# GpSimd's load queue in source order, and the projection products of the last three blocks one product later

## The chip, the core and the metric

The kernel runs on one core of one Trainium2 chip. A core has a TensorE (matrix products), a VectorE and a ScalarE (element by element work; the profile calls them DVE and ACT), a GpSimd (POOL), a SyncE (SP) and 16 DMA engines that all queues share. The metric is the time of one execution in microseconds, the median of several runs; lower is better.

## The reference

Attention over a sliding window, and then a gated feed-forward layer over its output. Shapes: 8 batches, 8 heads, 576 positions, head size 64; model width 512, inner width 1536.

```python
scores = 1/sqrt(64) * q @ k.T                       # each batch and head
mask = (rel >= 0) & (rel < 128)                     # rel = query position - key position
scores = where(mask, scores - slope[h] * abs(rel), -1e9)
attn = softmax(scores)
x = (attn @ v) as [8 * 576, 512]
out = (silu(x @ w_gate) * (x @ w_val)) @ w_out      # [4608, 512], float32
```

Inputs and output are float32.

## The kernel before

**Attention tiles.** The kernel works on 36 tiles of 128 positions, nine for each pair of batches: eight of 128 positions of one batch, and a ninth of the last 64 positions of both. Their number is called rank for inputs and i for work (`units`). For each tile, k, q and v are loaded with a conversion to float16 by DMAs that GpSimd issues (`load_qk` L187, `load_v` L182); the ninth tile of a pair takes two DMAs for each. From rank 11 on, k and q are transposed by DMAs of SyncE's queue (`transpose` L237, L243) into `kT` (12 places) and `qT` (9 places). `scores` makes the products of q and k (L282, L317), ScalarE the exponentials, VectorE applies masks; `weighted` multiplies with v (L349) and divides. Tile i's `weighted` needs v of i and mostly of i-1; the ninth tile also uses v of the fourth and the eighth. Loads of k and q pass through five buffers each (`nat`), which come free when the tile in them has been transposed; v has 12 places.

**What sets the order of loads.** The first eleven ranks are loaded by a list (L880 to L910), which mixes in the weights; after that, `loads_to(i + 7)` is called in tile i (L859), and `load` issues k, q, v for ranks below 10 and v, k, q after that. That is the order in the source. A planner then orders the instructions of each engine by its own costs and due times, except where `tc.manual_schedule` says that an engine's instructions stay in source order. Before, that holds for TensorE, VectorE and ScalarE in the first tiles, and for TensorE from step 60 on. GpSimd's and SyncE's queues are ordered by the planner. An engine takes its queue in order: an instruction that waits holds up all behind it. In GpSimd's queue the planner had put, for example, v of tiles 12, 13, 14 and 16 ahead of k of 12, v of 15 behind k of 23, and v of 33 at the very end.

**Feed-forward blocks.** Nine blocks n = 0 to 8 of 512 rows follow the attention in an interleaved way. Gate and value products of blocks 0 to 5 are plain (L401). For blocks 6 to 8 (`SEVEN_FROM`) each group of columns, a unit u = 0 to 5, takes seven half-size products instead of eight (`gate_val_by_seven`, L615, products at L627, in the banks gX, gY, gZ), with sums of x and weights made by VectorE (L489 to L492 for x, L601 to L604 for weights). `seven_steps` (L683) gives their order: in each unit first, seventh (of the unit before), fifth, sixth, fourth (of the unit before), second, third. A block has 42 such steps, k = 0 to 41. VectorE's adds L663 (after third) and L670 (after seventh) and its products L664 and L679 make hT, the block's inner activations.

**Projection.** The output product of blocks 1 to 8 is made by seven products as well (`strassen` L508, products at L536), twice for each block (t = 0, 1), so 14 steps of six matmuls of 256 columns: A11, A12, S2, S1, S3, S4, A22. Their sums of hT (S2, S3, S4 and S1 in place) are made by VectorE (`sums`, L489 to L492) from the finished hT. The projection of block n-1 is spread over block n: in blocks 7 and 8 (and for block 5's projection in block 6) one step follows each gate/value step with k % 3 == 1 (L753). The last block's own projection comes at the end (`ends`), its first step at k = 41. SyncE stores the results (`store`, L447) from eight `osb` buffers.

## Time and profile before

| What | Value |
|---|---|
| Median of 5 runs | 346.85 us (346.49 to 349.39) |
| The profiled execution's own time | 346.54 us |
| Its span in the profile | 344.8 us |
| TensorE matmul busy | 330.3 us, 96% |
| VectorE busy | 277.2 us, 80% |
| ScalarE busy | 207.6 us, 60% |
| GpSimd busy (issuing loads) | 109.9 us, 32% |
| Software DMA queue (q0), GpSimd's loads | 118336 packets, 18.62 MB, 84.0% of 16 engines |
| Hardware DMA queue (q1) | 40976 packets, 17.64 MB, 29.4% |

How to read it: busy time is the time in which an engine had an instruction in work; matmuls overlap, so their busy time can hide short waits, and the time from one matmul's start to the next tells more. A row of a timeline is: start in us from the start of the span, duration, engine, line, operation, output<-inputs, partitions x elements, and how many alike; in brackets, how long the engine had been idle before it and what ended that. GpSimd counts as busy while it issues a DMA; the transfer itself comes later.

### The profile page before, as it was taken

What the parts mean: (1) busy time and instruction counts of PE and PEld (TensorE: products, weight loads), DVE (VectorE), ACT (ScalarE), POOL (GpSimd) and SP (SyncE); (2) the same over time, 40 slices, a digit from 0 to 9 for tenths busy, and PEclk for the clock granted to TensorE, in tenths of its full rate; (3) what the DMA queues carried; (4) which work ended last, traced back from release to release, by engine and by line L of the source; (5) the groups of instructions that cost most, each with busy time, mean ns of one, the idle gap of its engine ahead of it and who ended that gap; (6) DMA issues with size and microseconds to landing.
All of it is one profiled execution on the core that took longest, in us unless ns stands there. A gap on an engine that the chain in (4) does not pass through costs nothing.

```text
span 344.8 us, 7788 instructions
## 1 busy us (share of the span) xinstructions
PE 330.3 (96%) x2983; PEld 218.7 (63%) x2983; DVE 277.2 (80%) x652; ACT 207.6 (60%) x412; POOL 109.9 (32%) x136
## 2 busy tenths in 40 slices
PE   7999989999999999999999999999999999999995
PEld 4484444444456565566565655565788878878884
DVE  6578885999798669998899999999855875775583
ACT  3758675465766665666555547563477667766750
POOL 8968695258558455634710000000000000000000
PEclk9999999999999999999999999999999999999999
DMA  9999999999999999999999312021101101011014
GB/s 152 169 180 175 159 176 167 103 138 138 158 146 144 170 172 136 178 124 177 151 164 165 94 29 80 15 63 47 63 7 56 63 0 64 20 43 63 0 64 122
DMA packets 160037, 37.37 MB, mean 108 GB/s; under 512 B 147328, under 2 KB 155648, under 8 KB 160000
## 3 DMA queue, kind: packets, MB, share of 16 engines
q0 software_dynamic: 118336, 18.62, 84.0%
q1 hardware_dynamic: 40976, 17.64, 29.4%
q10 hardware_dynamic: 688, 0.62, 0.6%
q8 instruction: 23, 0.38, 0.5%
q14 instruction: 14, 0.11, 0.1%
HBM read 37.91 MB, written 9.44 MB: 137 GB/s over the span
## 4 chain that ended last, share of the span: by engine, by line
PE 58%; DVE 22%; DMA 8%; ACT 6%; issue 4%; POOL 1%; SPq 0%; ACTq 0%; DVEq 0%; POOLq 0%
PE po L536 13%; PE pg L401 11%; PE pv L401 11%; PE gX L627 6%; PE av L349 3%; DVE hT L431 3%; PE gY L627 3%; DMA wo_sb<-in_moe_w_out_dram 3%; DVE uu L420 3%; PE ps L282 2%; DMA kT<-kn 2%; PE p L536 2%; DMA va<-in_v_dram 2%; DVE S L489 2%; DVE hT L490 2%
## 5 line engine op out<-in xcount | busy, mean ns | idle before, releaser
L401 PE MATMUL pv<-xT,wv_sb 128*128 128x512 f16 (+2 forms) x320 | 76.5, 358 | 0.6 <-DVE uu L420 0.3
L401 PE MATMUL pg<-xT,wg_sb 128*128 128x512 f16 (+2 forms) x320 | 75.8, 358 | 0.3 <-DVE xT L377 0.2
L419 ACT ACTIVATE tt<-pg 128x512 f16<-128x512 f32 (+2 forms) x70 | 41.3, 590 | 50.9 <-PE pg L401 49.9
L288 ACT ACTIVATE ex<-ps 128x512 f16<-128x512 f32 x96 | 50.0, 604 | 11.5 <-PE ps L282 11.5
L420 DVE SCALAR_TENSOR_TENSOR uu<-tt,pg 128x512 f16<-128x512 f16 (+2 forms) x69 | 45.9, 666 | 10.4 <-ACT tt L419 10.2
L431 DVE TENSOR_TENSOR hT<-uu,pv 128x512 f16<-128x512 f16 (+2 forms) x70 | 46.7, 666 | 3.6 <-PE pv L401 1.6
L191 POOL DMA_DIRECT2D kn<-in_k_dram x39 | 33.2, 854 | 34.7 <-DMA kT<-kn 24.2
L401 PEld LDWEIGHTS <-wg_sb 128*128 128x128 f16 x320 | 28.2, 98 | 24.4 <-issue 2.6
L401 PEld LDWEIGHTS <-wv_sb 128*128 128x128 f16 x320 | 28.3, 98 | 24.1 <-issue 3.0
L536 PEld LDWEIGHTS <-hT 128*128 128x128 f16 x384 | 36.9, 98 | 9.9 <-issue 1.1
L185 POOL DMA_DIRECT2D va<-in_v_dram x40 | 34.1, 856 | 16.4 <-PE av L349 7.2
L191 POOL DMA_DIRECT2D qn<-in_q_dram x39 | 33.3, 857 | 17.3 <-DMA qT<-qn 6.7
L536 PEld LDWEIGHTS <-S 128*128 128x128 f16 x288 | 27.6, 98 | 11.4 <-DVE S L491 2.6
L294 DVE TENSOR_TENSOR ex<-ex,m_reg 128x1024 f16<-128x1024 f16 x42 | 28.7, 687 | 3.2 <-ACT ex L288 3.1
L352 DVE TENSOR_TENSOR x<-av,rec 128x256 f16<-128x256 f32 x72 | 28.5, 420 | 0.4
L536 PE MATMUL po<-T,S 128*128 128x256 f16 x192 | 26.7, 273 | 1.5 <-DVE S L491 1.5
L536 PE MATMUL po<-T,hT 128*128 128x256 f16 x192 | 26.0, 273 | 0.0
L679 DVE TENSOR_TENSOR hT<-s,v 128x512 f16<-128x512 f16 x18 | 7.6, 423 | 21.4 <-ACT s L678 21.4
L321 ACT ACTIVATE exc<-psc 128x512 f16<-128x512 f32 x40 | 21.3, 607 | 3.7 <-PE psc L317 3.7
L349 PEld LDWEIGHTS <-ex 128*128 128x128 f16 x384 | 17.6, 97 | 5.4 <-issue 2.1
L349 PE MATMUL av<-va,ex 128*128 128x65 f16 x384 | 19.6, 193 | 1.3 <-ACT ex L288 0.7
L282 PE MATMUL ps<-qT,kT 64*128 64x256 f16 x192 | 16.6, 272 | 0.4 <-DVE qT L227 0.2
(134 smaller groups left out, 536.5 us busy)
## 6 DMA issues: line engine op xcount, KB each, us to landing
out_dram<-osb SPq DMA_DIRECT2D x32, 256.0 KB, 2.9
va<-in_v_dram POOLq DMA_DIRECT2D x32, 128.0 KB, 8.7
qn<-in_q_dram POOLq DMA_DIRECT2D x31, 128.0 KB, 8.0
kn<-in_k_dram POOLq DMA_DIRECT2D x31, 128.0 KB, 7.5
wg_sb<-in_moe_w_gate_dram POOLq DMA_DIRECT2D x6, 256.0 KB, 7.5
wv_sb<-in_moe_w_val_dram POOLq DMA_DIRECT2D x6, 256.0 KB, 8.1
wo_sb<-in_moe_w_out_dram POOLq DMA_DIRECT2D x2, 768.0 KB, 9.0
kn<-in_k_dram POOLq DMA_DIRECT2D x8, 64.0 KB, 9.9
```

The lines of the kernel that those rows point to most:

```text
L185: nc.gpsimd.dma_start(va[rank][p0:p1, :, 0:D], src)
L191: nc.gpsimd.dma_start(t_[p0:p1], src)
L288: nc.scalar.activation(e[:, o:o + 2, :], banks[q4][par], AF.Exp, scale=scale)
L294: nc.vector.tensor_mul(e[:, o, :], e[:, o, :], reg[:, o, :])
L349: nc.tensor.matmul(av[:, j, :], w, val, start=(n == 0), stop=(n == len(todo) - 1))
L352: nc.vector.tensor_mul(x[:, 4 * half:4 * half + 4, :], av[:, :, 0:D], rec.broadcast_to([P, 4, D]))
L401: nc.tensor.matmul(ps[:, c0:c1], w[:, kb, ms], xT[n][:, kb, c0:c1], start=(kb == 0 and c0 == 0), stop=(kb == NKB - 1 and c1 == 512), skip_ ...
L419: nc.scalar.activation(tt, pg[:, c0:c1], AF.Tanh, scale=0.5)
L420: nc.vector.scalar_tensor_tensor(out=uu, in0=tt, scalar=one if (n, m) == PIN else 1.0, in1=pg[:, c0:c1], op0=ALU.add, op1=ALU.mult)
L431: nc.vector.tensor_mul(hT[n][:, m, c0:c1], acted[(n, m)][1][:, c0:c1], pv[:, c0:c1])
L536: nc.tensor.matmul(dst, a[:, m, cols], b[:, m, :], start=(start and m == 0), stop=(m == HM - 1), skip_group_check=True)
L627: nc.tensor.matmul(dst[:, i, :], w[:, kb, c0 + i * P:c0 + (i + 1) * P], a[:, kb, :], start=(start and i == 0 and kb == 0), stop=(i == 1 an ...
```

## The change

Two parts. First, GpSimd's queue is put under `manual_schedule` from the first load on, so its DMAs stay in source order, and `load` issues k, q, v for every rank. With that, in GpSimd's queue each tile's loads stand together: v of 15 directly behind k and q of 15, and so on to v of 35 at the end; among the first eleven ranks only v of 0 and k of 2 change places, and v of 11 stands behind k and q of 11. SyncE's queue remains the planner's, which now alternates k and q transposes more strictly and places the stores differently between them. Second, the projection's steps in blocks 6 to 8 follow the gate/value steps with k % 3 == 2, one product later than before. The planner gives VectorE and ScalarE a slightly different order in these blocks. Nothing is added or removed: every engine has the same instructions.

```diff
     def load(rank):
-        if rank < 10:
-            load_qk(rank)
-            load_v(rank)
-        else:
-            load_v(rank)
-            load_qk(rank)
+        load_qk(rank)
+        load_v(rank)
...
             yield 0.5
-            if k % 3 == 1 and k < 42:
+            if k % 3 == 2 and k < 42:
                 next(parts)
                 yield 0.75
...
+    queue = ExitStack()
+    queue.enter_context(tc.manual_schedule(engines={ET.Pool}))
     load_qk(1, "qk")
     load_qk(2, "q")
...
     everything()
+    queue.close()
```

Order at the turn from block 6 to 7, TensorE, before: A22 of the projection before, third (6,5), first (7,0), seventh (6,5), A11, fifth, sixth, fourth (6,5), A12, second, third, first (7,1), S2, seventh (7,0), fifth, sixth, S1, fourth (7,0). After: third (6,5), A22 of the projection before, first (7,0), seventh (6,5), fifth, A11, sixth, fourth (6,5), second, A12, third, first (7,1), seventh (7,0), S2, fifth, sixth, fourth (7,0), S1.

## The prediction

> **What bounds the kernel now.** I read the page first, then who waited for whom on TensorE, then the chain of waits around the waits that the change can touch, then the timelines there. The page:

> ```profile
> span 344.8 us, 7788 instructions
> ...
> PE 330.3 (96%) x2983; PEld 218.7 (63%) x2983; DVE 277.2 (80%) x652; ACT 207.6 (60%) x412; POOL 109.9 (32%) x136
> ...
> DMA  9999999999999999999999312021101101011014
> ```

> TensorE is the bound, but its 96% hides short waits, so I use start-to-start times of matmuls: six of 256 columns take 0.66 us, four take 0.44, and what is longer is a stall. The DMA engines are full until about 190 us, the end of the loads. So the load queue matters only before 190, and only where a load arrives after TensorE wants it. All waits of TensorE for a DMA or for VectorE that lie in the change's reach:

> ```profile
> PE po L536 <- DVE S L491: 1.5, 3, 0.7
> ...
> PE av L349 <- DMA va<-in_v_dram: 0.6, 2, 0.3
> PE gX L627 <- DVE v L670: 0.6, 3, 0.2
> ```

> The columns are total us, times, longest. None exceeds a microsecond: little can be won. The timeline of TensorE places the two waits for v:

> ```profile
> 108.84 0.19 PE L349 MATMUL av<-va,ex 128*128 128x65 f16 x1
> 109.38 0.61 PE L349 MATMUL av<-va,ex 128*128 128x65 f16 x15 [0.34 <-DMA va<-in_v_dram]
> ...
> 165.79 0.61 PE L349 MATMUL av<-va,ex 128*128 128x65 f16 x15 [0.30 <-DMA va<-in_v_dram]
> ```

> A matmul of 65 columns follows the one before after 0.03 us, so the stalls are 109.38-108.84-0.03 = 0.51 us and, likewise from 165.29, 0.47 us. The chain of waits tells which counts:

> ```profile
> 92.20 7.60 DMA kT<-kn
> ...
> 102.93 6.41 DMA va<-in_v_dram
> ...
> 109.38 0.61 PE av L349 x15
> ...
> 163.66 1.00 ACT exc L321 x2
> ...
> 166.02 0.69 DVE exc L325
> ```

> The first v wait is on the chain, the second is not: there ScalarE's exponentials hold VectorE and the chain goes past the matmul. Counting TensorE's weighted sums, tile 15 starts at 108.84. Its v was issued at 102.93 only, because it stood in GpSimd's queue behind k tiles that waited for transposes. Tile 24 (165.29) is the same case.

> **Part A, the load queue.** It removes and adds no transfer; it puts 128 KB issues in the order k, q, v of each tile. The queue's timeline before:

> ```profile
> 59.50 0.88 POOL L185 DMA_DIRECT2D va<-in_v_dram  x1 [0.55 <-PE pv L401]
> 66.99 1.76 POOL L191 DMA_DIRECT2D kn<-in_k_dram  x2 [6.61 <-DMA kT<-kn]
> ...
> 102.93 2.65 POOL L185 DMA_DIRECT2D va<-in_v_dram  x3
> ...
> 180.09 0.89 POOL L185 DMA_DIRECT2D va<-in_v_dram  x1 [6.95 <-PE av L349]
> ```

> (1) v of 15 moves from 102.93 to behind q of 15, about 75 us: its buffer is that of tile 3, last read by tile 8's weighted sums at 67.19. Its stall goes: -0.51. v of 24 moves from 153.71 to just behind tile 17's sums (122.1), 43 us before its use. That stall goes too, but the chain passes elsewhere: I take -0.1, bounds 0 and -0.47.

> (2) What pays: k of 12 waits for the transpose of k of 11, and everything is queued behind it. Before, q of 12 and v of 12, 13, 14 and 16 went ahead of that wait (51.8 to 59.5); now they stand behind it. First to be missed is q of 12, read at 78.56 by scores. Before, the transpose was issued at 60.48 and held k of 12 until 66.99, with six younger loads in flight. Now only q and v of 11 are younger. The page has a transpose of 2.4 us with nothing beside it (`xT<-x`), so I take 59.6+2.4 to 3 = 62.0 to 62.6. [...] Then k of 12 at 62.5, q of 12 at 63.4 (0.87 an issue), landing 3.8 later (the least a kn load took is 3.4), its transpose issued behind k's (1.3 each on SP) at 67.8, landing 5 to 6 later (the first transpose's 5.9): 73 to 74, 5 us before use. [...] Cost 0. If k's transpose still ends at 66.4, q of 12 is ready at 78 to 79.5: a stall up to 1 us; with the worst qT landing, 9.8, about 83: 4.6.

> (3) Tiles 14 to 16 follow 1.3 to 2 us apart per transfer pair; read at 88.52, 94.75 and 99.78, they come at about 82, 86 and 90. Cost 0.

> (4) Head-of-line later: v of 24 waits for 122.1 and v of 33 for tile 26's sums (the 180.09 row). Behind v of 33 now stand k, q, v of 34 and 35: nine issues of 0.7 to 0.9, done at 187.5, landing and transposed by about 198. q of 34 is read at 212.35, so cost 0. [...] The trace has GpSimd's issues at 0.85 on the mean with VectorE above 90% busy at 60 to 80 us; I take the row. SP's stores stand behind fewer late transposes than before; osb has eight buffers. Cost 0. In the first ten us only k of 2 and v of 0 change places, 0.87 us; k of 2 is transposed at 12.48, after it landed at about 10. Cost 0.

> Sum of A: -0.6 (bounds -1.0 and +4.6).

> **Part B, the product order.** In blocks 6 to 8 each of the 14 projection products stands one gate/value product later. No product is added, and since 42 products hold each of the seven kinds at each place, mid-block spacings (one projection product between seventh and fourth, between first and sixth, between fourth and the next first) stay. What changes is the block's turn, where VectorE is behind:

> ```profile
> 275.87 0.60 PE L627 MATMUL gX<-xT,m_c 128*128 128x256 f16 x4 [0.18 <-DVE v L670]
> ...
> 279.52 0.39 PE L536 MATMUL po<-T,S 128*128 128x256 f16 x2 [0.66 <-DVE S L491]
> ...
> 281.06 0.82 PE L536 MATMUL po<-T,hT 128*128 128x256 f16 x6
> 281.72 0.60 PE L627 MATMUL gX<-xT,kT 128*128 128x256 f16 x4
> ```

> Stalls by pitch: 0.35 and 0.82 at this turn, 0.34 and 0.51 at the next (304.55, 307.89), 0.38 at 331.65 and 0.10 at 334.58 in the last block: 2.5 us, all for VectorE. If they all went, -2.5 is the bound. But I followed VectorE's queue in its new order with its row durations (0.33 pitch, 0.60 for the adds from PSUM, 0.12 more where an operation needs the one just before).
> - Turn 6 to 7: the add for the old unit's seventh starts at 274.7 instead of 275.13, so the fourth product need not wait (-0.35). TensorE would then run fourth 275.53, second 275.97, A12 276.41, third 277.06, first 277.50, seventh 277.94, S2 278.37, whose fifth matmul, at 278.81, needs the last S491. VectorE, after the four sums of x (275.7 to 277.4, as before): hT 277.4, the sum L490 277.8, osb 278.2, S491 278.5 to 278.9, then the add of third 278.8, S492 279.4, hT 279.8, the add of seventh 280.1 to 280.8. So 0.1 to 0.15 of the 0.82 stays. But the new block's fourth product, due at 280.05 (fifth and sixth, 0.87, after S2), needs that last add: a new stall of 0.8. Before, the S1 product (0.66) stood between. After both fourth and S1, TensorE is at 281.94 instead of 282.15: -0.2.
> - Turn 7 to 8: no sums of x in VectorE's queue there, so S2 does not wait; the new stall is 308.94-308.57 = 0.37. TensorE is at 310.03 instead of 310.52: -0.5.
> - End: the seventh stands earlier, the 0.38 goes, but the last S491 follows the same 23 operations with 0.17 more of dependence, and the projection's S2 waits for it: +0.15.

> B sums to -0.55, bounds -2.5 and +0.6 (the new stalls in full with nothing won at the first).

> **The sum.** -0.6-0.55 = -1.15 on the profiled execution: 346.54-1.15 = 345.4 (span 344.8 to 343.65; 1.7 lie around it). The median of the runs is 0.3 above the profiled one, so 345.7. About 0.5%, 1.7 us, is what a measurement tells from no change.

> **Rivals.** (R1) VectorE catches up and the turns lose their stalls: B -1.9, A -0.8, 344.1. For it: each turn's stall is under one product. Against: VectorE is busy without a gap from 268 to 280, so moving TensorE's order does not shorten it. (R2) Nothing moves: v waits turn into ScalarE waits (0.46 at 95.82 is one such), and the new stalls eat B: 346.8. For it: the chain at 166. (R3) Slower: the queue waits behind k of 12 and q of 12 comes after 78.56. It decides once that transpose lands after about 78.6, that is once k of 11's transpose ends after 66; its price is 1 to 4.6, and 14 and 15 follow late: about 348.7. For it: five transfers lose their place in an idle 6.6 us. Against: those five were the backlog that the transpose waited out.

> **How the numbers follow.** Chances: my sum 0.42 (own range 344.9 to 346.6), R1 0.26, R2 0.16, R3 0.16. The range of 344.0 to 347.6 holds R1's value, the sum, R2 and the cheap end of R3. Faster than 345.1: most of R1 and a quarter of the sum's case, 0.34. Slower than 348.6: half of R3 and what I overlooked, 0.18. Within: 0.48.

> **What would show it.** Right: no TensorE wait for v at tiles 15 and 24; k of 12 issued near 62.5; GpSimd idle before v of 24 and v of 33, six or more us each; a new wait of gX L623 (L627 before) for the add just after each turn, 0.4 to 0.8. Wrong: a wait of scores (L278, before L282) for qT or kT at 78 to 100; no new wait at the turns; the first loads or the SP stores holding an engine.

## The result, and the profile after

| | Before | After |
|---|---|---|
| Median | 347.54 us (346.01 to 349.39, 47 runs) | 346.23 us (345.55 to 348.94, 28 runs) |
| Span of the profiled execution | 344.8 us | 346.4 us |
| Its granted clock | 0.998 | 0.995 |

The ratio is 0.9973, with a 95% interval of 0.9957 to 0.9989: 0.9 us faster, 0.4 to 1.5. The two profiles seem to say the opposite, 1.6 us longer. That is the first thing to explain. The page after:

```profile
span 346.4 us, 7777 instructions
...
PE 330.8 (95%) x2983; PEld 219.7 (63%) x2983; DVE 276.9 (80%) x652; ACT 207.7 (60%) x412; POOL 110.0 (32%) x136
...
PEclk9999998999999999999999999999999999999999
DMA  9999999999999999999949925021101101011014
```

Busy times are those of before. New is the 8 in the seventh slice of the clock, 52 to 61 us. The waits of TensorE after, longest sum first (us in total, times, longest):

```profile
PE po L451 <- DMA wo_sb<-in_moe_w_out_dram: 2.0, 1, 2.0
PE po L532 <- DVE osb L536: 1.5, 2, 0.8
...
PE gX L623 <- DVE v L666: 0.9, 2, 0.6
...
PE po L532 <- DVE S L487: 0.5, 1, 0.5
```

The wait for v has gone from the list, and the wait of gX for the add after seventh is the new one that was forecast. But at the top stands a wait that the prediction did not discuss: an output product for the second half of the output weights, 0.7 us before and 2.0 now. The chain of waits after has it too, and no longer has v:

```profile
44.92 11.11 DMA wo_sb<-in_moe_w_out_dram
56.07 0.87 PE po L451 x2
...
109.86 0.86 PE pv L397 x4
110.72 0.86 PE pg L397 x4
111.58 0.48 PE av L345 x16
```

The half of the weights was issued at 44.92 and took 11.1 us; before it was 45.09 and 9.8. TensorE stood from 53.93 to 56.07 (2.15 us by start-to-start times, as stalls are counted throughout). Before, the same wait was 0.90 us:

```profile
53.64 0.59 PE L455 MATMUL po<-wo_sb,hT 128*128 128x512 f16 x2
54.97 0.59 PE L455 MATMUL po<-wo_sb,hT 128*128 128x512 f16 x2 [0.73 <-DMA wo_sb<-in_moe_w_out_dram]
```

After the wait of 2.15 us the clock fell. The columns of the next rows are the stretch in us, busy times of PE, PEld, DVE, ACT and POOL, the granted clock, the DMA share and GB/s:

```profile
56.00:57.00 1.00, 0.93 (x5) 0.50 (x5) 0.00 (x0) 0.00 (x0) 0.00 (x0) 0.62 2.42 154
57.00:58.00 1.00, 1.00 (x11) 0.95 (x9) 0.00 (x0) 0.38 (x1) 0.00 (x0) 0.50 2.42 154
58.00:59.00 1.00, 1.00 (x7) 0.49 (x5) 0.42 (x1) 0.20 (x1) 0.00 (x0) 0.50 2.12 135
59.00:60.00 1.00, 1.00 (x8) 0.63 (x7) 0.43 (x1) 0.59 (x1) 0.00 (x0) 0.67 0.58 36
60.00:61.00 1.00, 1.00 (x7) 0.41 (x6) 0.00 (x0) 0.62 (x2) 0.00 (x0) 1.00 0.18 29
```

Adding up what is missing to 1.00: 0.38 + 0.50 + 0.50 + 0.33 = 1.71 us of work lost, which is 3.4 us at half clock. So this execution holds 1.25 us of a longer wait and 1.7 us of half clock, 2.95 together, between 53 and 60 us. Both kernels have executions with a lower clock and without (below), and it explains the span: 344.8 + 2.95 = 347.75 would be the span without any gain, if nothing behind made up for a part, and it is 346.4.

TensorE at the places of the prediction, after:

```profile
111.42 0.65 PE L345 MATMUL av<-va,ex 128*128 128x65 f16 x16
...
167.45 0.65 PE L345 MATMUL av<-va,ex 128*128 128x65 f16 x16
...
171.33 0.81 PE L532 MATMUL po<-wo_sb,S 128*128 128x256 f16 x6 [0.63 <-DVE osb L536]
...
280.52 0.94 PE L532 MATMUL po<-T,S 128*128 128x256 f16 x6
...
282.93 0.60 PE L623 MATMUL gX<-xT,kT 128*128 128x256 f16 x4 [0.60 <-DVE v L666]
...
310.86 0.60 PE L623 MATMUL gX<-xT,kT 128*128 128x256 f16 x4 [0.26 <-DVE v L666]
```

The weighted sums of tiles 15 and 24 run in one piece of 16. At the turns, S2 (280.52) lasts 0.94 where six matmuls without a stall show 0.82, so 0.12 of its 0.82 us stall is left; the new stalls of the fourth product are 0.77 and 0.43 us (forecast 0.8 and 0.37). GpSimd's queue after:

```profile
51.11 0.90 POOL L185 DMA_DIRECT2D va<-in_v_dram  x1
62.65 0.88 POOL L191 DMA_DIRECT2D kn<-in_k_dram  x1 [10.64 <-DMA kT<-kn]
63.52 0.88 POOL L191 DMA_DIRECT2D qn<-in_q_dram  x1
...
125.41 0.88 POOL L185 DMA_DIRECT2D va<-in_v_dram  x1 [13.03 <-PE av L345]
...
182.25 0.88 POOL L185 DMA_DIRECT2D va<-in_v_dram  x1 [22.20 <-PE av L345]
```

k of tile 12 goes at 62.65 (forecast 62.5), and GpSimd idles 13 and 22 us before v of 24 and v of 33, as foreseen.

### The profile page after: what moved, and what is told of

Its sections match the earlier page's. It is cut to its first block, busy times and chain, and to the rows that moved or that the text cites. A ratio compares the mean times of both kernels' runs of the same rounds, so it can differ in the third digit from the quotient of the medians.

```text
span 346.4 us, 7777 instructions
## 1 busy us (share of the span) xinstructions
PE 330.8 (95%) x2983; PEld 219.7 (63%) x2983; DVE 276.9 (80%) x652; ACT 207.7 (60%) x412; POOL 110.0 (32%) x136
## 4 chain that ended last, share of the span: by engine, by line
PE 65%; DVE 17%; DMA 6%; POOL 5%; ACT 3%; issue 3%; DVEq 0%; ACTq 0%; POOLq 0%
PE po L532 14%; PE pv L397 12%; PE pg L397 12%; PE gX L623 8%; PE gY L623 4%; DMA wo_sb<-in_moe_w_out_dram 3%; PE av L345 3%; DMA qn<-in_q_dram 3%; DVE uu L416 3%; DVE hT L427 2%; PE p L532 2%; PE ps L278 2%; PE po L451 2%; PE gZ L623 2%; ACT ex L284 2%
## 5 line engine op out<-in xcount | busy, mean ns | idle before, releaser
L185 POOL DMA_DIRECT2D va<-in_v_dram x40 | 34.5, 867 | 42.1 <-PE av L345 36.2
L191 POOL DMA_DIRECT2D kn<-in_k_dram x39 | 33.4, 861 | 23.2 <-DMA kT<-kn 12.9
L191 POOL DMA_DIRECT2D qn<-in_q_dram x39 | 33.5, 865 | 12.0 <-DMA va<-in_v_dram 9.0
L345 PEld LDWEIGHTS <-ex 128*128 128x128 f16 x384 | 17.4, 97 | 4.6 <-issue 1.3
L345 PE MATMUL av<-va,ex 128*128 128x65 f16 x384 | 19.3, 193 | 0.7 <-ACT ex L284 0.7
L375 ACT COPY xT<-px 128x512 f16<-128x512 f16 x20 | 11.7, 584 | 8.9 <-PE px L371 8.7
```

The lines of the kernel that those rows point to most:

```text
L185: nc.gpsimd.dma_start(va[rank][p0:p1, :, 0:D], src)
L191: nc.gpsimd.dma_start(t_[p0:p1], src)
L345: nc.tensor.matmul(av[:, j, :], w, val, start=(n == 0), stop=(n == len(todo) - 1))
```

## The experiments

Three theories stood at the start. T: the two parts win what the sum says, 0.6 and 0.55 us, and the long wait for the output weights is a matter of chance in each execution. R1/R2 of the prediction: the turns, or the v waits, give more or nothing. R: the new load queue itself makes the weights late. Each fence has the line numbers of its own kernel: L345, L349 and L352 are the same line, and so are L451 and L455.

**The changed kernel again.** No edit.

> The changed kernel itself, taken again. The first profile of it is 346.4 us long with a granted clock of 0.995: its wait for the second half of the output weights (wo_sb) lasted 2.0 us at 56 us instead of 0.7, and the clock in the row of 55 to 60 us is 0.66. Theory T (wait and clock are a matter of chance in each execution, not of the change): a span of 344 +- 0.4 when the clock is 0.998 or more, with the stall at wo_sb at or under 1 us, and 346.2 to 347.1 when it is 0.994 or 0.995; ratio to the kernel before 0.995 to 0.999. Rival R (the new load queue makes the wait long every time): the wait is 2 us again, span 346.4.

346.80 us median (345.29 to 349.04, 15 runs), ratio 0.9977 (0.9953 to 1.0001). Its profile has the wait again, 2.21 us, at full clock:

```profile
56.29 0.59 PE L451 MATMUL po<-wo_sb,hT 128*128 128x512 f16 x2 [2.04 <-DMA wo_sb<-in_moe_w_out_dram]
```

So the wait of rival R is there again, but not its span: 345.4 us, 1.0 below the first profile. TensorE leaves the wait 0.2 us later than in the first profile and yet starts tile 15 at 110.16 instead of 111.42; of the 1.7 us of half clock, about 1.5 stayed in the time. With both sets, 43 executions of the changed kernel fall into three groups: 23 from 345.3 to 346.3, 11 from 346.8 to 347.4, and 9 from 348.2 to 349.0. All nine of the last group have a granted clock of 0.994 or 0.995; of the other 34 only one has, at 347.27. The steps between the groups fit the two sizes: about 1.2 for a wait of 2.2 in place of 0.9, and some 1.6 more for the half clock. The expectation of at most 1 us at full clock was wrong: long wait and half clock vary separately. That the wait is long every time (R) does not hold either, since 23 of 43 executions are in the lowest group.

**The queue alone, and the products alone.** One kernel has only the first part (the changed kernel with the line below), the other only the second (the kernel before with the same line turned round):

```diff
-            if k % 3 == 2 and k < 42:
+            if k % 3 == 1 and k < 42:
```

> Part A alone: GpSimd's load queue in source order, products at the old step. My sum: -0.6 us against the kernel before (ratio 0.998), no TensorE wait for v at tiles 15 and 24, and the five VectorE stalls at the turns as in the kernel before (0.35, 0.82, 0.34, 0.51, 0.38). Rival R2 (v waits turn into other waits): 0 (ratio 1.000), the stall of an output product behind tile 24's weighted sums grows by what the v wait loses (0.33 to 0.79, as the first profile of the changed kernel has it). Then half of A's gain is at tile 15 alone, 0.5.

> Part B alone: products one step later, the load queue as the planner orders it. My sum: -0.55 us (ratio 0.9984); by the stalls of the first profile of the changed kernel (0.77 and 0.43 at the turns and 0.43 at the end, in place of 0.35+0.82, 0.34+0.51, 0.38+0.10) it would be -0.8 (0.9977). k of tile 12 is issued near 67 and v of tile 15 near 103, as in the kernel before. If A and B add up, e2 and e3 sum to the change's ratio, 0.9973; if one alone gives it all, the other is 1.000.

The queue alone: 346.94 us, ratio 0.9987 (0.9969 to 1.0004); its profile has no wait for v. The products alone: 347.16 us, ratio 0.9983 (0.9962 to 1.0004). Each interval takes in 1, so neither is shown by itself here; their sum, 0.9970, is that of the change, 0.9973. The profile of the products alone, with the planner's load queue, has the short wait for the weights (1.00) and this at tiles 15 and 24:

```profile
108.93 0.19 PE L349 MATMUL av<-va,ex 128*128 128x65 f16 x1
110.65 0.61 PE L349 MATMUL av<-va,ex 128*128 128x65 f16 x15 [1.52 <-DMA va<-in_v_dram]
...
166.57 0.65 PE L349 MATMUL av<-va,ex 128*128 128x65 f16 x16
...
170.44 0.82 PE L536 MATMUL po<-wo_sb,S 128*128 128x256 f16 x6 [0.62 <-DVE osb L540]
```

The v wait of tile 15 is 1.69 us here, not 0.51: its size changes from one execution to the next. And tile 24 does not wait, but the output product 4 us later stalls by 0.79, where the kernel before had 0.47 and then 0.33. The sum is the same 0.8: the wait for v of 24 only eats into a later wait for VectorE.

**The output weights first.** The changed kernel, with the two halves issued one behind the other:

```diff
     nc.gpsimd.dma_start(wo_sb[:, 6:12, :], wo2[:, 6:12, :])
+    nc.gpsimd.dma_start(wo_sb[:, 0:6, :], wo2[:, 0:6, :])
     load_qk(9)
     load_qk(10, "q")
-    nc.gpsimd.dma_start(wo_sb[:, 0:6, :], wo2[:, 0:6, :])
```

> The changed kernel with the second half of the output weights issued directly behind the first half, ahead of k and q of tile 9 and q of tile 10. It lands near 51 to 53 instead of 55 to 56, before the product at 54 wants it; k and q of 9 and q of 10 land 4 us later, at 53 to 55, against uses at 54.5 to 55.7. Theory T (the late weights cause the stall and, when it is long, the drop of the clock, and with it the upper group of times at 348.2 to 348.9): no wait for wo_sb, no execution with a clock of 0.995, times 0.9 us below the lower group of the changed kernel, about 345.0, ratio 0.994. Rival R (the wait moves to the transposes of k and q of tile 9, which then land last): 346, ratio 0.997, with a wait of the transposes for DMA of about 1 us. Rival C (the clock drops by itself): some executions still at 0.995.

345.00 us (344.82 to 345.18, 6 runs), ratio 0.9916 (0.9888 to 0.9944). The groups are gone; the whole spread is 0.36 us. The second half lands at 53.23, and the products run on without a stall, four in one piece where the changed kernel had two and two:

```profile
53.94 1.02 PE L451 MATMUL po<-wo_sb,hT 128*128 128x512 f16 x4
54.80 0.28 PE L371 MATMUL px<-idm,x 128*128 128x128 f16 x2
54.91 0.39 PE L218 MATMUL pt<-idm,kn 128*128 128x128 f16 x4
```

The transposes of k and q of tile 9 wait 0.1 us at most. Six executions are few, but the three later kernels that have the weights first and the whole new queue add 24, and in none of the 30 is the clock under 0.998. So in the changed kernel the wait and the half clock came from this one transfer. Whether the new queue makes it late more often than the old one (a weaker form of R) stays open: the three profiles with the long wait all have the new queue, and the two of the old queue with the weights in their old place have the short one. That the kernel before has low clocks too, in 7 of 49 executions run beside the next kernels, does not settle it, because there the wait for v of tile 15 can be the cause (below: 5 of 22 with the weights first). What is gained for learning: with this wait away, smaller effects can be told apart. The next six kernels all have the weights first. Not all of them ran on the same chip; the kernel before, run beside each, has medians of 347.57, 347.52 and 347.44 us there, so differences between them are taken as good to about 0.1 us.

**Both parts undone on that base.** The first has the products at the old step, the second is the kernel before with the weights moved (so both parts undone).

> Output weights' second half issued behind the first, new load queue, but the products at the old step: against the run with both (345.0 us, 344.82 to 345.18) this gives part B with the wait for the weights out of the way. By the stalls in the profiles (0.35+0.82, 0.34+0.51 to 0.63, 0.38+0.1 in place of 0.77, 0.43, 0.43): 345.8 to 345.9. By my sum (-0.55): 345.55. Rival (B worth nothing once the weights are in time): 345.0.

> The kernel before with the second half of the output weights issued behind the first; load queue as the planner orders it, products at the old step. Against the kernel with the new queue and the old products (next to it in this call) it gives part A alone. With the v wait of tile 15 at 0.5 us (first profile of the kernel before): 0.5 above that one, 346.3, and with 1.7 (profile of the products alone): 347.5; a spread of about 1 us between executions, where the new queue has 0.4, if the time at which v of tile 15 lands is what varies. Rival (A worth nothing by itself, its earlier gain was that of the output weights): the same as its neighbour, 345.8, and as narrow.

Products at the old step: 345.74 us (345.42 to 346.06, 12 runs). Part B is 345.74 - 345.00 = 0.74 us, and the two spreads do not touch. Both undone: 347.42 us (345.83 to 352.26, 22 runs), so part A is 347.42 - 345.74 = 1.7 us on this base, almost four times what it gave before (0.45), and it takes the spread from 4.5 us (without the one execution at 352.26) to 0.6. The profile of the last shows why:

```profile
108.00 0.19 PE L349 MATMUL av<-va,ex 128*128 128x65 f16 x1
110.61 0.61 PE L349 MATMUL av<-va,ex 128*128 128x65 f16 x15 [2.41 <-DMA va<-in_v_dram]
```

v comes at 110.6, as in the products alone, but TensorE comes at 108.0 instead of 108.9, since it no longer waited at 54 us. It waits 2.6 us instead of 1.7. The weights first gain nothing in the old queue (347.42 against 347.52 for the kernel before): v does not come earlier when TensorE does, and its wait takes it all. That would also explain why the queue alone gave so little: an execution that is late from the weights has a shorter wait for v to lose.

**v of tile 15 by itself, both ways.** On the good base (both parts, weights first), v of 15 is asked for behind v of 21; and on the bad one (old queue and products, weights first), one tile earlier:

```diff
     def load(rank):
         load_qk(rank)
-        load_v(rank)
+        if rank != 15:
+            load_v(rank)
+        if rank == 21:
+            load_v(15)
```

```diff
         else:
-            load_v(rank)
+            if rank == 14:
+                load_v(15)
+            if rank != 15:
+                load_v(rank)
             load_qk(rank)
```

> The kernel with the weights first and both parts of the change, but v of tile 15 issued only behind v of tile 21, near 103 us, as the planner had it; no other order is touched. Theory (A's gain is this one wait): a TensorE wait for v at tile 15 of 0.5 to 1.7 us, and 345.5 to 346.7 us with a spread of about 1 us. Rival (A's gain comes from elsewhere in the queue, or the lost time is made up later): 345.0 to 345.2, as without the delay.

> The kernel before with the weights first (347.42 us, a TensorE wait of 2.6 us for v of tile 15 in its profile), and v of tile 15 alone asked for one tile earlier, which puts it ahead of k of tile 12 in the queue; all else as the planner orders it. Theory (v of tile 15 is all that part A wins): no wait at tile 15 and the time of the kernel with weights first, new queue and old products, 345.74, with its narrow spread (345.4 to 346.1). Rival (the new order wins elsewhere too): between 346.2 and 347.4.

Late: 349.57 us (346.94 to 353.64, 22 runs), 4.6 us more than without the delay. The forecast of 0.5 to 1.7 was too small: the profile has a stall of 2.64 us there with 1.7 us of half clock behind it, 4.3 of the 4.6, and 16 of the 22 executions have a clock of 0.995 or less. Early: 345.51 us (345.18 to 347.81, 15 runs), against 345.74 for the whole new queue with the same products. (In that kernel tile 8's sums read v of tile 15 for that of tile 3, since the place is written too soon. Its output is wrong, the amount of work is the same, and it serves for its times alone.) So, within the 0.2 us between these two, one transfer of 128 KB is all that part A wins in the typical execution. Three of the 15 are above 347, and one of these is the profiled one, with the whole wait at tile 24:

```profile
164.03 0.19 PE L352 MATMUL av<-va,ex 128*128 128x65 f16 x1
167.11 0.61 PE L352 MATMUL av<-va,ex 128*128 128x65 f16 x15 [2.88 <-DMA va<-in_v_dram]
...
170.16 0.82 PE L539 MATMUL po<-wo_sb,S 128*128 128x256 f16 x6
```

The stall is 3.05 us, and the one of the output product behind it is gone. The three profiles together have, for v of 24 and the output product: 0 and 0.79 (products alone), 0.47 and 0.33 (before), 3.05 and 0. So the first 0.8 us of a wait for v of 24 seem to cost nothing and the rest to cost in full: 3.05 - 0.79 = 2.3, and this execution is 2.3 above the median. A wait of this length for v of 24 is seen in this kernel only; in the profiles with the new queue v of 24 has no wait.

**What the new stall at the turn is made of.** Two steps on the good base. First, the sums of x for block 8, which the planner puts into VectorE's queue at the turn from 6 to 7, are held back to the middle of block 7, where the source has them, by a one-column copy whose result they overwrite:

```diff
+            held[:] = [s]
...
             if k == 20 and n + 1 < NBLK:
+                if n + 2 == NBLK:
+                    nc.scalar.copy(spare[3 * ((n + 1) % 2) + 1][:, 0, 0:1], held[0][:, 0, 0:1])
                 later.extend(x_sums(n + 1))
```

(`s` is the result of the activation that follows the fourth product, and `held[0]` the last of them.) Second, on top of it, ScalarE scales the second projection product:

```diff
-            nc.vector.tensor_scalar_mul(top[:, 0:HC], p2, factor)
+            nc.scalar.mul(top[:, 0:HC], p2, factor)
```

> The kernel with the weights first and both parts of the change, and the four sums of x for the last block held back: they run from step 20 of the block before it and not in VectorE's queue ahead of the turn from block 6 to 7 (a copy of one column by ScalarE, written over afterwards, is what holds them). Theory (the 0.77 us stall at the turn is VectorE's backlog, 1.8 us of it these sums): the add that the fourth product waits for comes 1.8 us earlier, the stall goes whole, 345.0 - 0.77 = 344.25. Rival (the stall is the dependence of the fourth product on the add just before it, 0.69 us of the add after the seventh, and stays at 0.4 as at the turn from 7 to 8): 344.65. Rival (the held sums make a stall in block 7): 345.0 or more.

> The kernel with the weights first, both parts of the change and the sums of x held back (344.69 us), and the scaling of the second projection product taken from VectorE's queue and given to ScalarE (six operations of 0.33 us). In that kernel 0.43 us stalls are left at both turns; the add that the fourth product waits for starts 1.2 us after its own product has ended, behind seven operations of VectorE, one of them this scaling. Theory (queue): each turn's stall shrinks by 0.33, to 0.10, and the time to 344.0. Rival (the 0.43 is the dependence of the fourth product on the add, whatever stands before it): 344.7, stalls unchanged. Rival (ScalarE's copies come later and make new waits): above 344.7.

The sums held back: 344.69 us (344.44 to 346.23, 6 runs, five of them below 344.9), 0.31 less; the stall at the turn from 6 to 7 went from 0.77 to 0.43, that of 7 to 8 stayed 0.43. The size is that of the rival, but not its mechanism. VectorE in that kernel:

```profile
275.84 0.43 DVE L676 TENSOR_TENSOR hT<-s,v 128x512 f16<-128x512 f16 x1 [1.17 <-ACT s L674]
276.30 0.42 DVE L486 TENSOR_TENSOR hT<-hT 128x512 f16<-128x512 f16 x1
276.64 0.42 DVE L547 TENSOR_SCALAR osb<-p 128x256 f32<-128x256 f32 x1
276.98 0.42 DVE L487 TENSOR_TENSOR S<-hT 128x512 f16<-128x512 f16 x1
277.31 0.69 DVE L659 TENSOR_TENSOR v<-gY,u 128x512 f16<-128x512 f32 x1
277.91 0.42 DVE L488 TENSOR_TENSOR S<-hT,S 128x512 f16<-128x512 f16 x1
278.24 0.42 DVE L660 TENSOR_TENSOR hT<-s,v 128x512 f16<-128x512 f16 x1
278.58 0.69 DVE L666 TENSOR_TENSOR v<-gX,p 128x512 f16<-128x512 f32 x1
```

VectorE had been idle for 1.17 us: most of the 1.8 us that the sums left free was lost to a wait for ScalarE. From there seven operations without a gap stand ahead of the add (L666), whose product (seventh, at 276.93) had long ended. It is still VectorE's queue. The second kernel takes the L547 row out: 344.23 us (344.03 to 344.95, 6 runs), ratio to the kernel before 0.9888 (0.9845 to 0.9931). The add comes at 278.42, and each turn's stall is 0.22: 0.21 less, not 0.33. The row of L487 now starts 0.46 behind L486, on which it depends, where the row between had hidden 0.12 of that. This is the best of the kernels here, 3.2 us under the kernel before.

**Work in place of the wait for the weights.** The changed kernel, weights late as they were, and six output products done twice ahead of the one that waits:

```diff
                 m = NMB - 1 - i if n == 0 else i
+                if (n, j, i) == (0, 0, 6):
+                    for r in range(6):
+                        nc.tensor.matmul(po, hT[n][:, NMB - 1 - r, 0:P], wo_sb[:, NMB - 1 - r, :],
+                                         start=(r == 0), stop=False)
...
-                                 start=(i == 0), stop=(i == NMB - 1))
+                                 start=(i == 0), stop=(i == NMB - 1 or (n, j, i) == (0, 0, 5)))
```

> The changed kernel, with six products of the first half of the output weights done twice, just ahead of the product that waits for the second half (1.3 us of work whose result is overwritten by nothing new: the same sum is formed again). The late weights are as late as ever. Theory (idle time of TensorE is what lowers the clock, and the weights matter only by that and by the wait itself): no execution with a clock of 0.995 and none above 347.6; executions with a short wait (0.9 us) take 0.4 to 0.6 more than the changed kernel's lower group, 346.4, those with a long one (2.2) the same as its middle group, 347.1. Rival (the clock falls for another reason at that place): still about one execution in five at 348.2 to 349.

346.12 us (345.88 to 346.73, 22 runs), ratio 0.9962 (0.9947 to 0.9978). No clock is under 0.997 in 22 executions, where the changed kernel had 10 of 43 at 0.994 or 0.995: with no idle stretch ahead of it the clock did not fall. The middle group, expected at 347.1, is missing as well, and the profile shows why:

```profile
56.00 0.59 PE L453 MATMUL po<-wo_sb,hT 128*128 128x512 f16 x2
...
66.46 1.46 PE L455 MATMUL po<-wo_sb,hT 128*128 128x512 f16 x6
```

The repeats (L453) stand, up to 56.4 us, where the products that need the second half stood; those products (L455) now come together at 66.46, ten microseconds after the latest landing seen, 56.4. So a late landing holds up nothing here, and these times do not tell when the weights come (54.93 in this profile). The expectation of what is left of a long wait was wrong about this. The kernel is only 0.2 us above the median of the changed kernel's lowest group, 345.9.

## Why the prediction was right, and where

Forecast 345.7 (344.0 to 347.6), measured 346.23; forecast -1.15 us, measured -0.9 (-1.5 to -0.4). The 0.3 us by which the forecast set the median above the profiled execution came from five runs; with 47 it is 1.0.

- **A1, the wait for v of 15 (-0.51).** It goes, and it is what the part wins. The size was read from one execution. It is 0.51, 1.69 and 2.58 us in three profiles with the old queue (before, products alone, weights first). Two things vary: v lands at 109.3 in the first and at 110.6 in the other two, and TensorE comes at 108.8, 108.9 and 108.0. The gain is 0.45 us (interval -0.1 to 1.1) in the kernel as it was, 1.7 with the weights first.
- **A1, v of 24 (-0.1).** Nothing for the 0.47 of the profile, and that by the chain of waits, as argued: the wait behind it grows from 0.33 to 0.79. That it can also be 3 us, as in one kernel above, was not foreseen.
- **A2, k and q of 12 (cost 0).** Right, step by step: the transpose of k of 11 issued 59.55 and landed 62.09, 2.5 us (forecast 2.4 to 3); k of 12 at 62.65, q of 12 at 63.52, landed 67.47 (4.0, forecast 3.8), its transpose issued 67.54 (67.8), landed 74.68 (73 to 74; 7.1 us instead of 5 to 6). Use was at 81.1 in this execution, 79.9 in the second and 78.05 with the weights first, where q of 12 is ready at 76.3: of the 5 us of cover, 1.7 are left, and rival R3 is next in line if anything else gets earlier. By the time of this transpose the queue of loads was nearly empty: the last load landed at 60.90, and the DMA share in the rows above is 0.58 from 59 to 60 us and 0.18 from 60 to 61, after 2.42 from 57 to 58. Before, the same transpose took 5.9 us. For the backlog as the cause of that speaks that it landed 0.5 us after the last of the loads issued ahead of it in all three profiles with the old queue: 66.42 after 65.90, 66.61 after 66.10, 67.02 after 66.52.
- **A3, A4 (cost 0).** Transposes of q of 14, 15 and 16 landed at 82.5, 87.1 and 92.9 (forecast 82, 86, 90), used at 91.1, 97.3 and 102.4. The issues behind v of 33 took 0.7 to 0.9 us each, and the last of them ended at 190.3 (forecast 187.5). No product waited for these loads.
- **Start (cost 0).** The profile after has a stall of 0.77 us at 27 us, for q of tile 5, where before had 0.44. It is 0.77 and 0.78 in two profiles of the new queue and 0.44 in the others, and it shows in two with the old queue as well (0.7 and 0.8): not the swap. It also cost nothing: by 28.2 us the two profiles of the changed kernel are within 0.04 us of each other.
- **B (-0.55).** Measured 0.74 in medians. TensorE's stalls in the profiles with the weights first, old products and new: turn 6 to 7, 1.17 to 0.87, -0.30 (forecast -0.2); turn 7 to 8, 0.86 to 0.43, -0.43 (-0.5); end, 0.52 to 0.62, +0.10 (+0.15). These make 0.63; the rest, 0.1, is within the spread of the executions. R1, VectorE catches up, fell: at the turns the new stalls came at the places and in the sizes forecast. At the end the size is right but not the place: 0.43 of it stands at the product A12, which waits for hT, and only 0.14 at S2.
- **The step that failed**, though the forecast held, is the first, "what bounds the kernel now". Its list of waits was cut to those "in the change's reach", and so left out the wait for the output weights, 0.7 us in the chain of before, on the ground that the change does not touch it. It is the largest term that varies between executions, 0.9 to 2.3 us and now and then 1.7 us of half clock on top, and by making TensorE late or not it helps to set what A is worth. That the sum came out near is partly luck: it set 0.51 for a v wait that two profiles of the same load queue show at 0.51 and 1.69.

## What to carry to other kernels

Waits of one engine for transfers that do not come earlier when the engine does, one behind the other, don't add: removing the first lengthens the second, removing the second pays little while the first varies, and removing both paid 1.8 us here (347.5 to 345.74, products unchanged) where each alone paid 0.1 and 0.45. Before you price a wait from one profile, look whether the times of the executions fall into groups: the spread of 3 us in this kernel of 347 was mostly waits for two transfers, whose length changed from one execution to the next. A stall on a queue that is full shrinks by what you take out of it in front, less the dependences and the waits for other engines that this uncovers: 1.8 us of sums taken out gave 0.34, and 0.33 of scaling gave 0.21.

## What the runs showed of the hardware that was not expected

The clock of TensorE fell to half for 3.41 us after a wait of about 2 us: in the profile after (stall 2.15), with the queue alone (2.31), and with v of 15 late (2.64). It did not after 2.21, 2.58 and 3.05 in three others. The fall came after the wait, when TensorE worked again: at 56.25 us in the profile after (resumed at 56.07), and at 112.10 with v of 15 late (resumed at 110.74), as the clock of these two rows has it:

```profile
111.00:112.00 1.00, 1.00 (x19) 0.88 (x16) 0.85 (x3) 0.00 (x0) 0.88 (x1) 1.00 1.97 156
112.00:113.00 1.00, 1.00 (x5) 0.38 (x3) 0.97 (x4) 0.00 (x0) 0.00 (x0) 0.55 1.67 186
```

The second 768 KB of the output weights, issued between 44.8 and 45.4 us, landed at 54.9 to 55.0 us in three profiles and at 56.0 to 56.4 in three others. One of the early ones has the same loads in the same order around it as the late ones. What decides it was not found.
